# Attention with a gate: row sums of the exponentials taken by ScalarE, P V without its column of ones

## The chip, the core and the metric

The kernel runs on one NeuronCore of a Trainium2 chip. Its engines work side by side, each with its own queue of instructions: TensorE (PE, and PEld for its weight loads), VectorE (DVE), ScalarE (ACT), GpSimd (POOL) and SyncE (SP), which here only issues DMAs. The metric is the device time of one launch in microseconds (us): 788.58 us, the median of three runs (788.07 to 789.41) of the kernel before the change.

## The reference

2048 tokens of width 640 are normalised to `xn`. Attention of 32 heads with 192 columns each looks at a window of the last 512 rows of the key and value caches; its output goes through `wo`, is multiplied by a gate and added to the input:

```python
W = min(4096, max(256, Sk // 4))                 # 512
q = (xn @ wq) per head;  k, v = last W rows of the caches
scores = einsum("bhqd,bhkd->bhqk", q, k) * Dh ** -0.5
p = softmax(scores);  s = einsum("bhqk,bhkd->bhqd", p, v) @ wo
# B: the two tokens with the highest xn @ w_r get a feed-forward update
g = silu(xn + update)
out = x + s * g
```

silu(x) is x times the logistic function of x, which is x (tanh(x/2)/2 + 1/2).

## The kernel before, in words

The queries of two heads (a pair) and 512 tokens make one of 64 steps, and half a step, 256 tokens, is one of 128 blocks. A block has two score tiles, a = 0 and a = 1, of 128 tokens for both heads. `wo` is applied over groups of four heads (two pairs), and adds into `s_acc`.

The order of the work is written out by hand. Blocks 0 to 11 (`HEAD = 12`) are threaded into the start of the kernel by the list `FIRST`, blocks 12 to 125 run in a loop over `BLOCK = "A S0 M0 W m E0 B S1 M1 P E1 l"`, and the list `LAST` holds the end. Each engine executes its instructions in this order. The tokens are:

- A and B: the two halves of a projection of queries for the next step (`q_phase`, L331), and behind B ScalarE's copy of the result out of PSUM (L343).
- S0, S1: the scores of a tile (`scores`, L358). There are two PSUM buffers for score tiles, so S0 of a block needs that E0 of the block before has read its tile, and likewise S1.
- M0, M1: VectorE's row maximum (`row_max`, L363).
- E0, E1: ScalarE's exponentials, two instructions of 128x512 for the two heads (`exps`, L380). Behind each pair SyncE issues a DMA that transposes the result (`pT`, L386).
- W: the product with `wo` for a block six earlier (`w_item`, L467), and two VectorE instructions that add it to `s_acc` (L500).
- P: P V of the block two earlier (`o_products`, L423): 32 matmuls, 16 for each of the two halves of the array (`r`), which run side by side, so 16 pairs. The moving operand is `v_ring[..., 0:Dh + 1]`, 193 columns, of which the last holds a constant 2.0. So column 192 of the result is twice the sum of the exponentials of its row. `o_scaled` takes its reciprocal on VectorE (L430, one instruction for each half) and multiplies it in: one half on ScalarE (L437, two instructions), one on VectorE (L434). Then SyncE issues the transposing DMA of the result (`oT`, L440). The result and W share two PSUM banks.
- m, l: other work that is due in this block, in particular DMA loads, GpSimd's copies (L119, L149) and the steps of the two-token update. Work in `bg` is emitted between the halves of P.

The gate (`gate_of`) is made of a ScalarE tanh (L897) and two GpSimd operations (L898, L899): tanh(x/2) x + x, which is twice silu. The factor two is undone by the 2.0 in the column of ones. It is called once for each of the 16 token tiles in blocks 28, 29, 45 to 53 and 56 to 60, and for the two chosen tokens in blocks 82 and 83. The two-token update is spread to all rows (`y_bc`) and added to the gates from block 85 on (L911, L912).

Of the kernel before, what the change touches and what calls it, by code (L numbers as in the profile page):

```python
# [8 lines left out]
ACT = mybir.ActivationFunctionType  # L9
ALU = mybir.AluOpType  # L10
AX = mybir.AxisListType
ET = mybir.EngineType
FP32 = mybir.dt.float32
# [8 lines left out]
def kernel(ctx, tc, A_x, A_k_cache, A_v_cache, A_wq, A_wo, B_x, B_w_r, B_w_gate, B_w_up, B_w_down, out):  # L22
    nc = tc.nc
    P = 128
# [3 lines left out]
    Dh = A_k_cache.shape[3]  # L28
# [10 lines left out]
    PAIRS = GROUP // 2  # L39
# [4 lines left out]
    scale = float(Dh) ** -0.5  # L44
# [12 lines left out]
    def pool(name, bufs, **kw):  # L57
        return ctx.enter_context(tc.tile_pool(name=name, bufs=bufs, **kw))

    const = pool("const", 1)  # L60
    big = pool("big", 1)
    small = pool("small", 4)
    wq_pool = pool("wq", 3)
    wo_pool = pool("wo", 4)
    kraw_pool = pool("kraw", 1)
# [8 lines left out]
    def f_tile(shape, dtype, name, kind="q"):  # L74
        return banks[kind].tile(shape, dtype, name=name, tag="f")
# [5 lines left out]
    RP, RO, RT, RV, VC = 3, 3, 7, 3, Dh + 8  # L81
    p_ring = big.tile([P, 2, 2, KB, 2, HK], BF16, name="pexp")
    pT_ring = big.tile([P, RP, 2, KB, P], BF16, name="pT")
    o_ring = big.tile([P, RO, CC, 2, HK], BF16, name="o_sb")
    oT_ring = big.tile([P, RT, CC, P], BF16, name="oT")
    v_ring = big.tile([P, RV, KB, VC], BF16, name="v_sb")
# [15 lines left out]
    def half(r):  # L102
        return slice(r * HK, (r + 1) * HK)
# [50 lines left out]
    for _ in range(13):  # L154
# [5 lines left out]
        out=ident_f, in_=ident_f, compare_op=ALU.not_equal, fill=1.0, base=0,  # L160
# [3 lines left out]
    eps_t = const.tile([P, 1], FP32, name="eps_t")  # L164
    nc.vector.memset(eps_t, EPS)
    nc.vector.tensor_copy(out=ident, in_=ident_f)
    nc.gpsimd.memset(v_ring[:, :, :, Dh:Dh + 1], 2.0)

    mv = const.tile([P, NTB, 2], FP32, name="mv")
    rstd = const.tile([P, NTB], FP32, name="rstd")  # L170
# [110 lines left out]
    HEAD = 12  # L281
# [32 lines left out]
    def q_phase(i, cs, ph):  # L314
        g, t5, pr = steps[i]
        if ph == 0:
            if banks["q"] is banks["o"]:
                q_ps = [f_tile([P, W], FP32, "q_ps") for _ in range(2)]
            else:
                q_ps = f_tile([P, 2, W], FP32, "q_ps")  # L320
            q_of[i, cs] = (q_ps, count["S"])
        else:
            assert last_max["S"] > q_of[i, cs][1]
        q_ps = q_of[i, cs][0]
        wq = grp[g][("wq", pr)]
        for dc in range(DC):
            for r in range(2):
                k = r if ph == 0 else 1 - r
                c, tok = (cs[k], slice(t5 * 4, t5 * 4 + 4)) if len(cs) == 2 else (cs[0], slice(t5 * 4 + 2 * k, t5 * 4 + 2 * k + 2))
                n = 512 if len(cs) == 2 else 256  # L330
                mm = nc.tensor.matmul(q_ps[k][:, 0:n] if type(q_ps) is list else q_ps[:, k, 0:n], lhsT=wq[half(r), dc, c:2 * Dh:3], rhs=xnT[half(r), tok, dc, :],  # L331
                                      start=(ph == 0 and dc == 0), stop=(ph == 1 and dc == DC - 1))
                if ph == 1 and dc == 0:
                    tc.add_manual_dep(mm.ins, last_max["ins"].name, mybir.DependencyInfo(mybir.DependencyClass.Sync, mybir.DependencyReason.DATA),
                                      reason="the banks change rows")
        if ph == 1:
            qT = q_tile(i)
            out = qT[:, cs[0]:cs[0] + 2, :] if len(cs) == 2 else qT[:, cs[0], :].rearrange("p (k t) -> p k t", k=2)
            if type(q_ps) is list:
                for k in range(2):  # L340
                    nc.scalar.activation(out=out[:, k], in_=q_ps[k][:, 0:n], func=ACT.Copy, scale=scale)
            else:
                nc.scalar.activation(out=out, in_=q_ps[:, :, 0:n], func=ACT.Copy, scale=scale)  # L343
# [3 lines left out]
    nm_of = {}  # L347

    def scores(b, a):
        i = b // 2  # L350
        g, t5, pr = steps[i]
        u = 2 * (b % 2) + a
        s_of[b, a] = ps_s.tile([P, 2, W], FP32, name="s", tag="sc")
        count["S"] += 1
        s_no[b, a] = count["S"]
        for c in range(3):
            for r in range(2):
                nc.tensor.matmul(s_of[b, a][:, r, :], lhsT=qT_of[i][half(r), c, u * P:(u + 1) * P],  # L358
                                 rhs=grp[g][("kT", pr)][half(r), :, c, :], start=(c == 0), stop=(c == 2))
# [5 lines left out]

    split_of = set()

    p_last = {}

    def p_of(b, a):  # L370
        if b < NB - 1:
            return p_ring[:, b % 2, a]
        if a not in p_last:
            t = wq_pool.tile([P, DC, 2 * Dh], BF16, name="wq_g")
            p_last[a] = t.rearrange("p c d -> p (c d)")[:, 0:KB * P].rearrange("p (k h e) -> p k h e", k=KB, h=2)
        return p_last[a]

    def exps(b, a, split=False):
        for hh in range(2):
            nc.scalar.activation(out=p_of(b, a)[:, :, hh, :].rearrange("p (x j) e -> p x j e", x=2),  # L380
                                 in_=s_of[b, a][:, hh, :].rearrange("p (j e x) -> p x j e", j=NJ, x=2),
                                 func=ACT.Exp, bias=nm_of[b, a][:, hh:hh + 1], scale=1.0)
        if a == 0 and split:
            split_of.add(b)
        if b in split_of:
            nc.sync.dma_start_transpose(out=pT_ring[:, b % RP, a], in_=p_of(b, a).rearrange("p k h e -> p (k h e)"))  # L386
        elif a == 1 and b < NB - 1:
            nc.sync.dma_start_transpose(out=pT_ring[:, b % RP].rearrange("p a k t -> p (a k) t"),
                                        in_=p_ring[:, b % 2].rearrange("p a k h e -> p (a k h e)"))
# [18 lines left out]

    o_of = {}

    def o_products(b, between=None, where="o"):
        g, t5, pr = steps[b // 2]
        if where == "o":
            o_of[b] = [f_tile([P, 2, W // 2], FP32, "o_ps", "o") for _ in range(2)]
        else:
            o_t = f_tile([P, 2, 2, W // 2], FP32, "o_ps") if where == "q" else ps_s.tile([P, 2, 2, W // 2], FP32, name="o_ps", tag="sc")
            o_of[b] = [o_t[:, r] for r in range(2)]
        for a in range(2):
            if a == 1 and between is not None:
                between()  # L420
            for k in range(KB):
                for r in range(2):
                    nc.tensor.matmul(o_of[b][r][:, a, 0:Dh + 1], lhsT=pT_ring[half(r), b % RP, a, k, :],  # L423
                                     rhs=v_ring[half(r), (g * PAIRS + pr) % RV, k, 0:Dh + 1],
                                     start=(k == 0), stop=(k == KB - 1))

    def o_scaled(b, engines):
        rl = small.tile([P, 2, 2], FP32, name="rl")
        for r, e in sorted(enumerate(engines), key=lambda c: c[1]):
            nc.vector.reciprocal(out=rl[:, r], in_=o_of[b][r][:, :, Dh])  # L430
            o_sb = o_ring[:, b % RO, 3 * r:3 * r + 3].rearrange("p c a e -> p a c e")
            src = o_of[b][r][:, :, 0:Dh].rearrange("p a (c e) -> p a c e", e=HK)
            if e == "v":
                nc.vector.tensor_tensor(out=o_sb, in0=src, in1=rl[:, r].unsqueeze(2).unsqueeze(3).to_broadcast([P, 2, 3, HK]), op=ALU.mult)  # L434
            else:
                for a in range(2):
                    nc.scalar.activation(out=o_sb[:, a], in_=src[:, a], func=ACT.Copy, scale=rl[:, r, a:a + 1])  # L437
# [457 lines left out]

    def gate_of(tz, x, y):
        nc.scalar.activation(out=tz, in_=x, func=ACT.Tanh, scale=0.5)  # L897
        nc.gpsimd.tensor_tensor(out=tz, in0=tz, in1=x, op=ALU.mult)  # L898
        nc.gpsimd.tensor_tensor(out=y, in0=tz, in1=x, op=ALU.add)  # L899

    def m_gate(n):
        def f():
# [83 lines left out]
    for b in range(HEAD, NB - 2):  # L986
        for token in BLOCK:
            if token in "AB":
                if b // 2 + 1 < NS:
                    q_phase(b // 2 + 1, ((0, 1), (2,))[b % 2], "AB".index(token))  # L990
            elif token[0] == "S":
                scores(b, int(token[1]))
            elif token[0] == "M":
                row_max(b, int(token[1]))
            elif token[0] == "E":
                exps(b, int(token[1]), split=True)
            elif token == "W":
                w_item(b - LAG)
            elif token == "P":
                def between():  # L1000
                    for f in bg.pop(b, []):
                        f()
                o_item(b - 2, "va", between)
            else:
                for f in mid.pop(b, []) if token == "m" else end.pop(b, []) + loads.pop(b, []):
                    f()

# [64 lines left out]
```

## Time and profile before

| | before |
|---|---|
| median of three runs | 788.58 us |
| the profiled execution | 788.91 us |
| its span, first to last instruction | 787.1 us |
| granted TensorE clock, mean | 0.999 |
| PE busy | 774.5 us (98%) |
| VectorE busy | 578.8 us (74%) |
| ScalarE busy | 527.9 us (67%) |
| GpSimd busy | 339.3 us (43%) |

A row of the groups reads: line, engine, operation, output<-inputs, shapes, count | busy time, mean ns of one | idle time of the engine before them, and what ended it. In the chain of waits each row is a start, a duration and the work that the end of the kernel stood on at that time. In the timeline a row is a start, a duration, and how many instructions were merged into it.

### The profile page before, as it was taken

The page shows a single profiled execution, that of the slowest core. Times are in us where ns is not written, and L with a number is a line of the kernel's source. Part 1 is how long each engine was busy: PE and PEld are TensorE (multiplying, and loading weights), DVE is VectorE, ACT ScalarE, POOL GpSimd, SP SyncE. Part 2 cuts the span into 40 slices and gives each one's busy share as a digit, 9 for nine tenths or more (in the row PEclk, how much of TensorE's full clock was granted, in tenths as well). Part 3 has the DMA queues.
Part 4 walks back from the last instruction along what each step waited for, and adds up shares of the span by engine and source line. Part 5 has one row for each costly group of instructions (what it writes and reads, how often), then busy time and mean ns, then how long its engine had stood idle before and what let it go on. Part 6 is the DMA issues. An engine that isn't in the chain of part 4 may idle for free.

```text
span 787.1 us, 27038 instructions
## 1 busy us (share of the span) xinstructions
PE 774.5 (98%) x11384; PEld 573.3 (73%) x11384; DVE 578.8 (74%) x1068; ACT 527.9 (67%) x956; POOL 339.3 (43%) x281
## 2 busy tenths in 40 slices
PE   8899999999999999999999999999999999999997
PEld 4457677777777777777777777777777777777776
DVE  7898788887787766767767776767767677677675
ACT  6676666667666677767666666766666666666663
POOL 1334110023120236527120101569987696165897
PEclk9999999999999999999999999999999999999999
DMA  9989999899999999999999999999999899999994
GB/s 237 195 174 174 168 193 167 141 195 163 163 211 177 182 201 194 192 171 198 184 194 191 185 216 187 161 193 174 177 168 183 144 170 188 179 193 150 193 190 109
DMA packets 447130, 142.18 MB, mean 181 GB/s; under 512 B 414180, under 2 KB 446438, under 8 KB 447008
## 3 DMA queue, kind: packets, MB, share of 16 engines
q1 hardware_dynamic: 437456, 130.96, 100.5%
q10 hardware_dynamic: 8528, 6.64, 3.4%
q0 software_dynamic: 1024, 2.85, 1.4%
q8 instruction: 89, 1.46, 0.8%
q14 instruction: 33, 0.27, 0.1%
HBM read 40.31 MB, written 2.63 MB: 55 GB/s over the span
## 4 chain that ended last, share of the span: by engine, by line
PE 92%; DVE 3%; DMA 2%; ACT 2%; issue 0%; SPq 0%; DVEq 0%; ACTq 0%
PE w L467 26%; PE q_ps L331 24%; PE o_ps L423 21%; PE s L358 20%; DVE nm L363 1%; PE q_ps L300 1%; ACT pexp L380 1%; DMA oT<-o_sb 1%; DMA x_in<-in_A_x_dram 1%; DMA v_sb<-in_A_v_cache_dram 1%; PE tp L274 0%; ACT o_sb L437 0%; ACT xnT L275 0%; PE gu_ps L821 0%; DVE stats L523 0%
## 5 line engine op out<-in xcount | busy, mean ns | idle before, releaser
L363 DVE TENSOR_REDUCE nm<-s 128x2 f32<-128x1024 f32 x256 | 313.1, 1224 | 137.6 <-PE s L358 135.8
L380 ACT ACTIVATE pexp<-s,nm 128x512 bf16<-128x512 f32 x508 | 321.6, 688 | 95.2 <-DVE nm L363 91.5
L331 PE MATMUL q_ps<-xnT,wq_g 64*128 64x512 bf16 (+1 forms) x2340 | 232.6, 323 | 0.0
L467 PE MATMUL w<-wo_g,oT 64*128 64x320 bf16 x3072 | 231.4, 296 | 0.2
L358 PE MATMUL s<-kT,qT 64*128 64x512 bf16 x1536 | 211.5, 376 | 2.1 <-ACT pexp L380 1.8
L467 PEld LDWEIGHTS <-oT 64*128 64x128 bf16 x3072 | 171.0, 94 | 57.9 <-DMA oT<-o_sb 0.7
L423 PEld LDWEIGHTS <-pT 64*128 64x128 bf16 x4096 | 177.6, 94 | 30.1 <-issue 2.8
L423 PE MATMUL o_ps<-v_sb,pT 64*128 64x193 bf16 x4096 | 195.2, 243 | 2.3 <-DMA pT<-pexp 1.2
L437 ACT ACTIVATE o_sb<-o_ps,rl 128x192 bf16<-128x192 f32 x250 | 91.6, 417 | 130.6 <-DVE rl L430 127.7
L331 PEld LDWEIGHTS <-wq_g 64*128 64x128 bf16 x2340 | 125.8, 99 | 45.8 <-DVE qT L304 0.5
L149 POOL COPY wo_g<-wo_g 64x1920 bf16<-64x1920 bf16 x32 | 57.2, 1792 | 189.4 <-DMA wo_g<-in_A_wo_dram 151.2
L358 PEld LDWEIGHTS <-qT 64*128 64x128 bf16 x1536 | 84.9, 94 | 56.9 <-issue 2.8
L500 DVE TENSOR_TENSOR s_acc<-s_acc,w 128x320 f32<-128x320 f32 x192 | 85.0, 484 | 31.4 <-PE w L467 31.3
L343 ACT ACTIVATE qT<-q_ps 128x1024 bf16<-128x1024 f32 x114 | 92.4, 811 | 7.0 <-PE q_ps L331 0.8
L434 DVE TENSOR_TENSOR o_sb<-o_ps,rl 128x384 bf16<-128x384 f32 x131 | 73.0, 557 | 4.5
L119 POOL COPY k_perm<-k_raw 128x768 bf16<-128x768 bf16 x30 | 24.3, 826 | 93.9 <-DMA k_raw<-in_A_k_cache_dram 67.9
L911 POOL TENSOR_SCALAR yh<-y_bc,oh 128x640 f32<-128x640 f32 x32 | 60.3, 1883 | 5.0 <-DMA y_bc<-y_d 2.3
L912 POOL TENSOR_TENSOR xn<-xn,yh 128x640 bf16<-128x640 bf16 x32 | 44.9, 1404 | 2.7
L898 POOL TENSOR_TENSOR tz<-tz,xn 128x640 f32<-128x640 f32 x16 | 22.4, 1398 | 54.8 <-ACT tz L897 54.8
L430 DVE RECIPROCAL rl<-o_ps 128x2 f32<-128x2 f32 x256 | 30.7, 160 | 11.7 <-PE o_ps L423 6.3
L971 POOL TENSOR_TENSOR s_acc<-s_acc,x_fin 128x640 f32<-128x640 f32 x16 | 22.4, 1398 | 10.9 <-DMA x_fin<-in_A_x_dram 9.9
L899 POOL TENSOR_TENSOR xn<-tz,xn 128x640 bf16<-128x640 f32 x16 | 22.4, 1398 | 1.3
(141 smaller groups left out, 275.8 us busy)
## 6 DMA issues: line engine op xcount, KB each, us to landing
wo_g<-in_A_wo_dram SPq DMA_DIRECT2D x32, 240.0 KB, 4.2
k_raw<-in_A_k_cache_dram SPq DMA_DIRECT2D x32, 192.0 KB, 3.5
v_sb<-in_A_v_cache_dram SPq DMA_DIRECT2D x32, 192.0 KB, 4.1
wq_g<-in_A_wq_dram SPq DMA_DIRECT2D x14, 288.0 KB, 4.0
pT<-pexp SPq DMA_TRANSPOSE x246, 4.1
wq_g<-in_A_wq_dram SPq DMA_DIRECT2D x14, 192.0 KB, 2.9
x_fin<-in_A_x_dram SPq DMA_DIRECT2D x16, 160.0 KB, 3.6
oT<-o_sb SPq DMA_TRANSPOSE x126, 3.6
```

What stands on the lines that cost most here:

```text
L149: nc.gpsimd.tensor_copy(out=grp[g][("wo", pr)][half(1), cs, :], in_=grp[g][("wo", pr)][half(0), cs, :])
L331: mm = nc.tensor.matmul(q_ps[k][:, 0:n] if type(q_ps) is list else q_ps[:, k, 0:n], lhsT=wq[half(r), dc, c:2 * Dh:3], rhs=xnT[half(r), tok ...
L343: nc.scalar.activation(out=out, in_=q_ps[:, :, 0:n], func=ACT.Copy, scale=scale)
L358: nc.tensor.matmul(s_of[b, a][:, r, :], lhsT=qT_of[i][half(r), c, u * P:(u + 1) * P], rhs=grp[g][("kT", pr)][half(r), :, c, :], start=(c = ...
L363: rm = nc.vector.tensor_reduce(out=nm_of[b, a], in_=s_of[b, a], axis=AX.X, op=ALU.max, negate=True)
L380: nc.scalar.activation(out=p_of(b, a)[:, :, hh, :].rearrange("p (x j) e -> p x j e", x=2), in_=s_of[b, a][:, hh, :].rearrange("p (j e x) - ...
L423: nc.tensor.matmul(o_of[b][r][:, a, 0:Dh + 1], lhsT=pT_ring[half(r), b % RP, a, k, :], rhs=v_ring[half(r), (g * PAIRS + pr) % RV, k, 0:Dh ...
L434: nc.vector.tensor_tensor(out=o_sb, in0=src, in1=rl[:, r].unsqueeze(2).unsqueeze(3).to_broadcast([P, 2, 3, HK]), op=ALU.mult)
L437: nc.scalar.activation(out=o_sb[:, a], in_=src[:, a], func=ACT.Copy, scale=rl[:, r, a:a + 1])
L467: nc.tensor.matmul(w_ps[r][:, 0:cs.stop - cs.start], lhsT=oT_ring[half(r), bs[pr] % RT, c, :], rhs=grp[g][("wo", pr)][half(r), c, cs], sta ...
L500: nc.vector.tensor_tensor(out=acc, in0=acc, in1=src, op=ALU.add)
L911: nc.gpsimd.tensor_scalar(out=yh, in0=M["y_bc"][:, j, :], scalar1=M["oh"][:, n, j:j + 1], scalar2=None, op0=ALU.mult)
```

## The change

From block 12 on `exps` passes `accum_out`: each ScalarE instruction writes, beside the exponentials, their sum over its 512 elements into one column of a small tile `l` (five buffers, for the two token tiles and two heads of a block). VectorE takes one reciprocal of the four columns of `l` (`o_factor`), in token m of the block in which P of that `l` stands; in the list `LAST` it is taken in `o_scaled`. P V from block 12 on has 192 columns. The ScalarE and VectorE multiplications of `o_scaled` read the result of P and this reciprocal. Blocks 0 to 11 keep the column, which now holds 1.0. The gate becomes x (tanh(x/2)/2 + 1/2): the first GpSimd operation is a `tensor_scalar` with two constants in place of a `tensor_tensor`, and the second one multiplies where it added. The order of the matmuls and of the DMA issues is as it was.

```diff
-    nc.gpsimd.memset(v_ring[:, :, :, Dh:Dh + 1], 2.0)
+    nc.gpsimd.memset(v_ring[:, :, :, Dh:Dh + 1], 1.0)
...
     def exps(b, a, split=False):
+        if b >= HEAD and a == 0:
+            l_of[b] = sums.tile([P, 2, 2], FP32, name="l")
         for hh in range(2):
             nc.scalar.activation(out=p_of(b, a)[:, :, hh, :].rearrange("p (x j) e -> p x j e", x=2),
                                  in_=s_of[b, a][:, hh, :].rearrange("p (j e x) -> p x j e", j=NJ, x=2),
-                                 func=ACT.Exp, bias=nm_of[b, a][:, hh:hh + 1], scale=1.0)
+                                 func=ACT.Exp, bias=nm_of[b, a][:, hh:hh + 1], scale=1.0,
+                                 accum_out=l_of[b][:, hh, a:a + 1] if b >= HEAD else None)
...
+    def o_factor(b):
+        rl_of[b] = small.tile([P, 2, 2], FP32, name="rl")
+        nc.vector.reciprocal(out=rl_of[b], in_=l_of[b])
+
     def o_products(b, between=None, where="o"):
+        n = Dh if b >= HEAD else Dh + 1
...
-                    nc.tensor.matmul(o_of[b][r][:, a, 0:Dh + 1], lhsT=pT_ring[half(r), b % RP, a, k, :],
-                                     rhs=v_ring[half(r), (g * PAIRS + pr) % RV, k, 0:Dh + 1],
+                    nc.tensor.matmul(o_of[b][r][:, a, 0:n], lhsT=pT_ring[half(r), b % RP, a, k, :],
+                                     rhs=v_ring[half(r), (g * PAIRS + pr) % RV, k, 0:n],
                                      start=(k == 0), stop=(k == KB - 1))
 
     def o_scaled(b, engines):
-        rl = small.tile([P, 2, 2], FP32, name="rl")
+        if b >= HEAD and b not in rl_of:
+            o_factor(b)
+        rl = rl_of[b] if b >= HEAD else small.tile([P, 2, 2], FP32, name="rl")
         for r, e in sorted(enumerate(engines), key=lambda c: c[1]):
-            nc.vector.reciprocal(out=rl[:, r], in_=o_of[b][r][:, :, Dh])
+            if b < HEAD:
+                nc.vector.reciprocal(out=rl[:, r], in_=o_of[b][r][:, :, Dh])
...
     def gate_of(tz, x, y):
         nc.scalar.activation(out=tz, in_=x, func=ACT.Tanh, scale=0.5)
-        nc.gpsimd.tensor_tensor(out=tz, in0=tz, in1=x, op=ALU.mult)
-        nc.gpsimd.tensor_tensor(out=y, in0=tz, in1=x, op=ALU.add)
+        nc.gpsimd.tensor_scalar(out=tz, in0=tz, scalar1=0.5, scalar2=0.5, op0=ALU.mult, op1=ALU.add)
+        nc.gpsimd.tensor_tensor(out=y, in0=tz, in1=x, op=ALU.mult)
...
             else:
+                if token == "m" and b - 2 >= HEAD:
+                    o_factor(b - 2)
```

More of the change, by code (lines that the diff above doesn't have):

```diff
@@ L62 @@
     small = pool("small", 4)
+    sums = pool("sums", 5)
     wq_pool = pool("wq", 3)
@@ L366 @@
     split_of = set()
+    l_of = {}
+    rl_of = {}
     p_last = {}
```

## The prediction

> **What bounds the kernel now.** I read the engines' busy time first, then the chain of waits, then the timeline of two blocks and of the end.
>
> ```profile
> span 787.1 us, 27038 instructions
> PE 774.5 (98%) x11384; PEld 573.3 (73%) x11384; DVE 578.8 (74%) x1068; ACT 527.9 (67%) x956; POOL 339.3 (43%) x281
> PE 92%; DVE 3%; DMA 2%; ACT 2%; issue 0%; SPq 0%; DVEq 0%; ACTq 0%
> ```
>
> The chain stands on matmuls for 92% of the span. A busy PE need not be PE at its pace, so the stages themselves have to be looked at. This is the chain inside the loop, and one row of it from a worse place:
>
> ```profile
> 156.34 0.65 PE s L358 x6
> 156.99 1.63 PE w L467 x24
> 158.62 1.08 PE q_ps L331 x10
> 159.70 0.65 PE s L358 x6
> 160.34 1.33 PE o_ps L423 x32
> 161.68 0.55 PE q_ps L331 x10
> ...
> 216.25 1.80 PE w L467 x24
> ```
>
> One stage follows the other with nothing between. Matmuls come in pairs, one for each half of the array. W has 12 pairs of 320 columns in 1.63 us, 136 ns a pair; the projection has 5 pairs of 512 columns in 1.08 us, 216 ns; P has 16 pairs of 193 columns in 1.33 us, 83 ns. From P to W that is 53 ns for 127 columns, from W to the projection 80 ns for 192: 0.417 ns for a column both times. So these stages go by their columns, and PE has no waits in the loop except for single cases such as 1.80 us for W at 216.25. Nearly all that other engines do is hidden behind PE, and the change is worth what it takes from PE's columns, unless it makes another engine late.
>
> **P with 192 columns.** From block 12 on there are 116 blocks with 16 pairs each: 116 x 16 x 0.417 ns = 0.77 us less on PE, all of it on the path. The two ends are 0 (the pair is paced by something else than columns, a rival below) and 0.80 (time in proportion to columns, 1.33 us / 193 for each). I take 0.77, because the slope comes out the same from two intervals.
>
> **The sums on ScalarE.** A sum needs an instruction that reads it out. This kernel has such reads in its start, behind row sums of another kind:
>
> ```profile
> 58.45 1.26 ACT L380 ACTIVATE pexp<-s,nm 128x512 bf16<-128x512 f32 x2
> 59.59 0.83 ACT L538 ACTIVATE xn<-x_in,sums 128x640 bf16<-128x640 bf16 x1
> 60.31 0.20 ACT L538 ACTIVATION_READ_ACCUMULATOR xn<-x_in,sums 128x1 f32 x1
> 60.40 0.83 ACT L538 ACTIVATE xn<-x_in,sums 128x640 bf16<-128x640 bf16 x1
> ```
>
> The read is recorded with 0.20 us but overlaps on both sides. Two exponentials of 1.26 us are followed after 1.14 us, so an instruction overlaps the next by 0.12. Without the read, the one at 59.59 would be followed after 0.83 - 0.12 = 0.71 us; it was followed after 0.81. The read costs 0.10 us. It can't cost less than nothing, since no work leaves ScalarE with it; the upper end is the whole 0.20 with the overlaps on both of its sides lost, about 0.40. I take 0.10, the measured one: 0.2 us for each pair of exponentials, 0.4 us a block. Whether that is hidden is read from a pair of blocks in which the tanh of a gate makes ScalarE busiest:
>
> ```profile
> 304.35 0.24 DVE L430 RECIPROCAL rl<-o_ps 128x2 f32<-128x2 f32 x2
> 304.56 0.42 ACT L437 ACTIVATE o_sb<-o_ps,rl 128x192 bf16<-128x192 f32 x1 [0.54 <-DVE rl L430]
> 304.88 0.41 ACT L437 ACTIVATE o_sb<-o_ps,rl 128x192 bf16<-128x192 f32 x1
> 305.18 1.27 ACT L380 ACTIVATE pexp<-s,nm 128x512 bf16<-128x512 f32 x2
> 305.34 1.81 PE L467 MATMUL w<-wo_g,oT 64*128 64x320 bf16 x24
> 306.87 1.27 ACT L380 ACTIVATE pexp<-s,nm 128x512 bf16<-128x512 f32 x2 [0.43 <-DVE nm L363]
> 308.03 0.60 ACT L343 ACTIVATE qT<-q_ps 128x512 bf16<-128x512 f32 x1
> 308.51 0.74 ACT L897 ACTIVATE tz<-xn 128x640 f32<-128x640 bf16 x1
> 309.49 1.26 PE L331 MATMUL q_ps<-xnT,wq_g 64*128 64x512 bf16 x10
> 309.71 0.24 DVE L430 RECIPROCAL rl<-o_ps 128x2 f32<-128x2 f32 x2
> 309.92 0.73 ACT L437 ACTIVATE o_sb<-o_ps,rl 128x192 bf16<-128x192 f32 x2 [0.66 <-DVE rl L430]
> 311.22 2.06 PE L467 MATMUL w<-wo_g,oT 64*128 64x320 bf16 x24
> ```
>
> E1 at 305.18 gets 0.2 longer and starts up to 0.2 earlier (below), so it ends where it did; behind it ScalarE waits 0.43 us for the row maximum, and E0 at 306.87 starts as before. E0's 0.2 moves the copy of the queries from 308.03 to 308.23; it ends at 308.83, and PE needs its bank back at 309.49. The tanh ends at 309.45 in place of 309.25, and ScalarE waited until 309.92 for the reciprocal, 0.66. What stands behind the exponentials (the DMA pT that SyncE issues, the score buffer that PE refills) gets the 0.2 as well: the buffer read from 306.87 to 308.14 is refilled by the scores ahead of W at 311.22, 0.65 us earlier, at 310.57, which leaves 2.4 us. If this cover were gone, 0.2 a pair would be 0.4 us a block or 46 us in all; it isn't. Cost on the path: 0.
>
> **The reciprocal.** It leaves the place between P and `o_scaled`. ScalarE's L437 starts 0.21 us after the first L430 (304.35, 304.56), and without it starts that much earlier: when P is done. VectorE's half gains the 0.24 of two. The result is out of PSUM 0.2 us sooner, W finds its banks free sooner (at 305.34 they had been free for 0.05 us: 304.88 + 0.41 = 305.29), and SyncE may issue oT sooner. PE did not wait there, so this is worth nothing in the loop, but it pays for E1's longer time. The new reciprocal of four columns, 0.12 to 0.24 us by the row of two, lies on VectorE in front of the maximum M1:
>
> ```profile
> L363 DVE TENSOR_REDUCE nm<-s 128x2 f32<-128x1024 f32 x256 | 313.1, 1224 | 137.6 <-PE s L358 135.8
> ```
>
> VectorE waits for scores for 135.8 us ahead of these 256, 0.53 us each, which covers it; the sum it reads was written a block earlier. 0.
>
> **The gate.** GpSimd's first operation changes its kind:
>
> ```profile
> L898 POOL TENSOR_TENSOR tz<-tz,xn 128x640 f32<-128x640 f32 x16 | 22.4, 1398 | 54.8 <-ACT tz L897 54.8
> L911 POOL TENSOR_SCALAR yh<-y_bc,oh 128x640 f32<-128x640 f32 x32 | 60.3, 1883 | 5.0 <-DMA y_bc<-y_d 2.3
> L185 POOL TENSOR_SCALAR xn<-x_in,rstd,nmr 128x640 bf16<-128x640 bf16 x7 | 6.4, 919 | 6.4 <-DVE nmr L189 6.4
> ...
> 522.01 0.83 POOL L119 COPY k_perm<-k_raw 128x768 bf16<-128x768 bf16 x1 [0.42 <-DMA k_raw<-in_A_k_cache_dram]
> 541.58 1.54 SPq L123 DMA_TRANSPOSE kT<-k_perm  x1
> ```
>
> It is between 0.48 us shorter (L185) and 0.49 longer (L911, the nearer in type) than 1.40. With 16 gates GpSimd waits 54.8 us for the tanh, 3.4 each, which covers it. With the two of blocks 82 and 83 the spread of the update and GpSimd's copies of keys behind it come up to 1 us later; the transposing DMA that reads them is issued 18.7 us after them. 0.
>
> **The end.** Here the chain leaves PE for once:
>
> ```profile
> 770.39 0.61 PEld L405 LDWEIGHTS <-wq_g 64*128 64x128 bf16 x32
> 770.69 0.17 DVE L430 RECIPROCAL rl<-o_ps 128x2 f32<-128x2 f32 x1 [0.40 <-PE o_ps L423]
> 770.89 0.73 ACT L437 ACTIVATE o_sb<-o_ps,rl 128x192 bf16<-128x192 f32 x2 [0.50 <-DVE rl L430]
> 770.94 1.51 PE L423 MATMUL o_ps<-v_sb,pT 64*128 64x193 bf16 x32
> 771.66 0.17 DVE L430 RECIPROCAL rl<-o_ps 128x2 f32<-128x2 f32 x1 [0.80 <-ACT o_sb L437]
> 771.87 0.56 DVE L434 TENSOR_TENSOR o_sb<-o_ps,rl 128x384 bf16<-128x384 f32 x1
> 772.57 1.81 PE L467 MATMUL w<-wo_g,oT 64*128 64x320 bf16 x24
> ```
>
> P of block 126 at 770.94 takes 1.33 us, so W could start at 772.27; it starts at 772.57, since its bank is freed by the VectorE half of block 125 at 771.87 + 0.56 = 772.43. Both reciprocals go from in front of it, 0.20 and 0.21 us. Then the bank is free at 772.02, ahead of PE: 0.30 us gained (0 if something else holds W).
>
> **Sum.** 0.77 + 0.30 = 1.07 us less. The profiled execution took 788.91, of which the span is 787.1; it would take 787.84. It lies 0.33 above the median of the runs, so against the median of 788.58 I say 787.5, which is 0.14% faster. About 0.2% (1.6 us) is what a measurement of this kernel can tell from no change, so this falls within it.
>
> **Rivals.**
>
> The column buys nothing. P could be paced by its weight loads, of which there are as many after as before:
>
> ```profile
> L423 PEld LDWEIGHTS <-pT 64*128 64x128 bf16 x4096 | 177.6, 94 | 30.1 <-issue 2.8 <-DMA pT<-pexp 1.4 <-DMA v_sb<-in_A_v_cache_dram 0.7
> ```
>
> For it speaks that a load lasts 94 ns, longer than the 83 ns of a pair. Against it: the 32 loads at 770.39 were done in 0.61 us, 38 ns a pair, so loads overlap each other, and P lies on the line of the other stages. Then only the end is gained: 788.3. The Trainium skill has such a rule (TensorE: Matmul & The Clock Gate, "Back-to-back issue gap" and "LDWEIGHTS"): the spacing in a stream of loads and matmuls is set by both, and a load takes its columns over 1.2 in ns. An estimate from that page for the 128 columns here is 107 ns, 1.71 us for 16 in a row; the trace's 1.33 us does not agree.
>
> Waits shrink too. Banks are free 0.2 us sooner and oT may be issued sooner; W at 216.25 lost 0.17 us and W at 311.22 lost 0.25 (2.06 against 1.81). If both vanish and other small ones with them, 0.5 to 0.8 us more are gained: 786.9. Against it: W at 311.22 waits for a DMA, and SyncE issues that in its own order.
>
> Slower: the read does not overlap in front of exponentials. At 0.40 us each, E1 ends 0.8 - 0.2 later, 0.17 more than the 0.43 it may; E0 ends 0.17 + 0.8 later, and the copy of the queries at 309.60, 0.11 past the 309.49 at which PE wants the bank. The point is 4 reads = 0.43 + 0.2 + 0.86, or 0.37 us a read. With 58 pairs of blocks that is 6 us, and the tanhs add to it: 794. Against it is the measured 0.10.
>
> **How the numbers follow.** My forecast has 0.64, with 787.0 to 788.1 as its own range; the column that buys nothing 0.10; waits that shrink 0.16; the late ScalarE, or another engine made late in its manner, 0.10. The range from 786.5 to 788.9 takes in the first three and leaves out the last and a little below. Faster by over 0.2%, under 787.0: 0.18, the third with the lower edge of the first. Slower: 0.12, the fourth and a little of the scatter. Within: 0.70.
>
> **What the profile will show.** P of 32 matmuls at 1.32 to 1.33 us in the chain; a read of about 0.2 us behind each exponential, pairs of exponentials 1.45 to 1.5 us from start to end of the read; L437 waiting for PE and no longer for L430; ScalarE busy near 73% (464 reads of 0.10 us more); W in the end at 772.27 less what was gained before. I am wrong if the query copies end after PE wants their bank, if the scores wait for ScalarE in the loop, or if P keeps 83.3 ns a pair to the last digit.

## The result

The changed kernel takes 785.51 us (median; 785.36 to 786.62) beside 788.80 before. The ratio is 0.9961, with an interval from 0.9948 to 0.9973: faster by 0.39%, some 3.1 us (3.3 between the medians), where 1.07 us were forecast. The range began at 786.5, so the time lies below it.

The page of the changed kernel, its first lines, and the rows of the groups that the change touches:

```profile
span 784.0 us, 27247 instructions
...
PE 771.7 (98%) x11384; PEld 572.0 (73%) x11384; DVE 561.2 (72%) x952; ACT 566.2 (72%) x1420; POOL 327.1 (42%) x281
...
L452 ACT ACTIVATE o_sb<-o_ps,rl 128x192 bf16<-128x192 f32 x250 | 91.6, 418 | 97.3 <-PE o_ps L435 88.3 <-DVE rl L445 6.9 <-DMA pT<-pexp 1.0
...
L386 ACT ACTIVATION_READ_ACCUMULATOR pexp<-s,nm 128x1 f32 x460 | 94.0, 204 | 0.0
...
L386 ACT ACTIVATION_READ_ACCUMULATOR wq_g<-s,nm 128x1 f32 x4 | 0.8, 210 | 0.0
...
L913 POOL TENSOR_SCALAR tz<-tz 128x640 f32<-128x640 f32 x16 | 11.7, 728 | 63.7 <-ACT tz L912 63.7
```

All 464 reads are there: 460, and four whose exponentials go to a buffer of another name. ScalarE's half of P's result waits for PE now and hardly for a reciprocal; ScalarE is busy 72% of the span. GpSimd's first gate operation takes 0.73 us.

The chain of waits in the loop, around the same two places as before:

```profile
156.03 0.65 PE s L359 x6
156.68 1.63 PE w L482 x24
158.31 1.08 PE q_ps L332 x10
159.39 0.65 PE s L359 x6
160.04 1.32 PE o_ps L435 x32
161.36 0.55 PE q_ps L332 x10
...
215.38 1.63 PE w L482 x24
```

P takes 1.32 us, and W at 215 is back at 1.63 us from 1.80. To say what made up the 3.1 us, I divided each profile at the same matmuls: the head up to the first score matmul of block 13, the loop from there to the first one of block 126 (113 blocks), and the tail. Single waits are those matmuls of the loop that start over 40 ns later behind the one before than nearly all of their kind do, summed over the excess. All from the start times of matmuls, in us:

| | P columns, reciprocal | head | loop | single waits in it | loop without them | tail | span |
|---|---|---|---|---|---|---|---|
| before | 193, behind P | 91.40 | 668.85 | 1.01 | 667.84 | 26.89 | 787.14 |
| changed | 192, early | 91.28 | 666.26 | 0.40 | 665.86 | 26.50 | 784.04 |

Of 3.10 us the loop without single waits gives 1.98, single waits 0.61, the tail 0.39 and the head 0.12. The experiments take the loop and the tail apart.

### The profile page after: what moved, and what is told of

It reads as the page before. It is cut to its first block, busy times and chain, and to the rows that moved or that the text cites. A ratio compares the mean times of both kernels' runs of the same rounds, so it can differ in the third digit from the quotient of the medians.

```text
span 784.0 us, 27247 instructions
## 1 busy us (share of the span) xinstructions
PE 771.7 (98%) x11384; PEld 572.0 (73%) x11384; DVE 561.2 (72%) x952; ACT 566.2 (72%) x1420; POOL 327.1 (42%) x281
## 4 chain that ended last, share of the span: by engine, by line
PE 93%; DVE 4%; ACT 2%; DMA 0%; issue 0%; DVEq 0%; ACTq 0%
PE w L482 26%; PE q_ps L332 24%; PE o_ps L435 21%; PE s L359 20%; DVE nm L364 1%; PE q_ps L301 1%; ACT pexp L386 1%; DMA x_in<-in_A_x_dram 0%; DVE stats L538 0%; DVE o_sb L449 0%; ACT xnT L276 0%; DVE qT L305 0%; PE gu_ps L836 0%; PE tp L275 0%; DVE stats L248 0%
## 5 line engine op out<-in xcount | busy, mean ns | idle before, releaser
L386 ACT ACTIVATE pexp<-s,nm 128x512 bf16<-128x512 f32 x508 | 342.6, 688 | 94.7 <-DVE nm L364 91.0
L435 PE MATMUL o_ps<-v_sb,pT 64*128 64x192 bf16 (+1 forms) x4096 | 193.7, 243 | 2.8 <-DMA pT<-pexp 1.6
L386 ACT ACTIVATION_READ_ACCUMULATOR pexp<-s,nm 128x1 f32 x460 | 94.0, 204 | 0.0
L913 POOL TENSOR_SCALAR tz<-tz 128x640 f32<-128x640 f32 x16 | 11.7, 728 | 63.7 <-ACT tz L912 63.7
```

Of the source, the lines that this page charges most:

```text
L435: nc.tensor.matmul(o_of[b][r][:, a, 0:n], lhsT=pT_ring[half(r), b % RP, a, k, :], rhs=v_ring[half(r), (g * PAIRS + pr) % RV, k, 0:n], star ...
```

## The experiments

Three kernels were built between the two: the gate alone, then the sums without their use, then the early reciprocal with P still at 193 columns; the changed kernel is the last step.

**The gate alone.** The kernel before with

```diff
-    nc.gpsimd.memset(v_ring[:, :, :, Dh:Dh + 1], 2.0)
+    nc.gpsimd.memset(v_ring[:, :, :, Dh:Dh + 1], 1.0)
...
-        nc.gpsimd.tensor_tensor(out=tz, in0=tz, in1=x, op=ALU.mult)
-        nc.gpsimd.tensor_tensor(out=y, in0=tz, in1=x, op=ALU.add)
+        nc.gpsimd.tensor_scalar(out=tz, in0=tz, scalar1=0.5, scalar2=0.5, op0=ALU.mult, op1=ALU.add)
+        nc.gpsimd.tensor_tensor(out=y, in0=tz, in1=x, op=ALU.mult)
```

> The kernel before with the new gate alone (and the column of ones at 1.0). GpSimd's first operation went from 1.40 to 0.73 us. Theory: it is hidden, so 788.8 us within 0.3, and the single long W stages of the loop (1.80 us at 216, 2.06 at 311) stay. Rival: a shorter GpSimd operation relieves these waits, up to 0.6 us: 788.2.

**The sums, not used.** The same, with `accum_out` in `exps` from block 12 on; P and the reciprocals as before:

```diff
+                                 accum_out=l_of[b][:, hh, a:a + 1] if b >= HEAD else None)
...
         rl = small.tile([P, 2, 2], FP32, name="rl")
             nc.vector.reciprocal(out=rl[:, r], in_=o_of[b][r][:, :, Dh])
```

> The kernel before with the new gate and with the sums taken on ScalarE but not used: P keeps 193 columns and the reciprocals are taken from PSUM behind P as before. Against the run with 193 columns it differs in the place of the reciprocal alone, against the gate alone in the reads of ScalarE. Theory: the early reciprocal frees W's banks sooner and that is where 1 to 1.5 us came from, so this is 788.8 us or up to 0.5 more, with the start of W behind the scores alternating as before (about 0.20 and 0.21 us behind the last score matmul). Rival: the reads themselves shift the DMA issues into better places, then 787.5 or less.

**The early reciprocal, 193 columns.** The changed kernel with

```diff
-        n = Dh if b >= HEAD else Dh + 1
+        n = Dh + 1
```

> The changed kernel with P at 193 columns again (the last is not used); all else of the change stays. It tells what the column alone is worth. Theory now: TensorE takes columns in twos, so 193 cost as much as 194, and the P stage of 32 matmuls goes back from 1.32 us to 1.333 us: 116 blocks x 13.4 ns = 1.55 us, 787.1 us beside 785.5. Theory of the prediction, 0.417 ns for one column: 786.3 us, and the P stage at 1.327 us or lower. If the sums and the early reciprocal did nothing, the time would be that of before, 788.8; I expect the other 1.6 us to stay gained.

What the three gave, beside 789.08 us for the kernel before on the same chip:

| | median | ratio to before, interval | head | loop | single waits | loop without | tail |
|---|---|---|---|---|---|---|---|
| gate alone | 788.87 | 0.9998 (0.9988 to 1.0007) | 90.94 | 669.16 | 1.35 | 667.81 | 26.78 |
| with sums, unused | 789.11 | 0.9996 (0.9985 to 1.0008) | 93.23 | 668.25 | 0.48 | 667.77 | 26.87 |
| early reciprocal, 193 | 787.74 | 0.9985 (0.9975 to 0.9994) | 91.34 | 668.35 | 1.00 | 667.35 | 26.52 |
| changed | | | 91.28 | 666.26 | 0.40 | 665.86 | 26.50 |

The row of the changed kernel is its profile from the result above; it did not run beside the other three. The gate and the reads on ScalarE change the loop without single waits by 0.03 and 0.04 us: they are hidden. The two long W stages, expected to stay with the gate alone, are not in its profile; P at 309 us waited 0.87 us there instead, for the transposing DMA of `pT`.

The place of the reciprocal is worth 0.42 us in the loop and 0.35 in the tail, the column 1.49 in the loop: 13.2 ns for each of 113 blocks, 0.82 ns for each pair of matmuls. That is two columns at 0.417 ns, not one. These steps repeat: over all profiles of these kernels and of those below with equal widths, the loop without single waits is 667.77 to 667.84 us with 193 columns and the reciprocal behind P, 667.35 and 667.36 with 193 and the early one, and 665.86 to 665.89 with 192.

The medians differ by more than the parts found in the profiles: 1.37 us for the place of the reciprocal, of which 0.77 are located, and 2.0 to 2.2 for the column (the changed kernel has 785.51 above and 785.75 below) where 1.55 were expected. What the executions without a profile waited for is not known. The heads differ by up to 2.3 us between kernels whose first 12 blocks do the same, so one profile tells nothing of a head.

**P at several widths.** The changed kernel, with the columns behind 192 set and not used:

```diff
-        n = Dh if b >= HEAD else Dh + 1
+        n = Dh + ((0, 1, 2, 3, 4, 5, 6, 8)[b // 2 % 8] if b >= HEAD else 1)
...
-    nc.gpsimd.memset(v_ring[:, :, :, Dh:Dh + 1], 1.0)
+    nc.gpsimd.memset(v_ring[:, :, :, Dh:VC], 1.0)
```

> The changed kernel with P at 192, 193, 194, 195, 196, 197, 198 and 200 columns, by step modulo 8 (the columns past 192 are not used), so that one trace gives the price of each. In twos: the stage of 32 matmuls lasts 1.320 us with 192, 1.333 with 193 and 194, 1.347 with 195 and 196, 1.360 with 197 and 198, 1.373 with 200. One by one at 0.417 ns: 192 at 1.320, then 6.7 ns more for each column, 1.327 at 193 and 1.333 at 194. Paced by the weight loads: the same for all.

The timeline of PE, start of P and of the projection behind it, at 198, 200, 192, 193, 194, 195 and 196 columns:

```profile
106.55 1.54 PE L435 MATMUL o_ps<-v_sb,pT 64*128 64x198 bf16 x32
107.91 1.25 PE L332 MATMUL q_ps<-xnT,wq_g 64*128 64x512 bf16 x10
...
112.99 1.55 PE L435 MATMUL o_ps<-v_sb,pT 64*128 64x200 bf16 x32
114.36 0.72 PE L332 MATMUL q_ps<-xnT,wq_g 64*128 64x256 bf16 x10
...
131.04 1.50 PE L435 MATMUL o_ps<-v_sb,pT 64*128 64x192 bf16 x32
132.36 1.26 PE L332 MATMUL q_ps<-xnT,wq_g 64*128 64x512 bf16 x10
...
142.79 1.51 PE L435 MATMUL o_ps<-v_sb,pT 64*128 64x193 bf16 x32
144.12 1.26 PE L332 MATMUL q_ps<-xnT,wq_g 64*128 64x512 bf16 x10
...
154.56 1.51 PE L435 MATMUL o_ps<-v_sb,pT 64*128 64x194 bf16 x32
155.89 1.26 PE L332 MATMUL q_ps<-xnT,wq_g 64*128 64x512 bf16 x10
...
166.34 1.53 PE L435 MATMUL o_ps<-v_sb,pT 64*128 64x195 bf16 x32
167.68 1.26 PE L332 MATMUL q_ps<-xnT,wq_g 64*128 64x512 bf16 x10
...
178.13 1.52 PE L435 MATMUL o_ps<-v_sb,pT 64*128 64x196 bf16 x32
179.48 1.26 PE L332 MATMUL q_ps<-xnT,wq_g 64*128 64x512 bf16 x10
```

1.36, 1.37, 1.32, 1.33, 1.33, 1.34 and 1.35 us. Over all such stages of the trace the medians in ns are 1320 at 192; 1333 and 1333 at 193 and 194; 1347 and 1346 at 195 and 196; 1360 and 1360 at 197 and 198; 1373 at 200 (13 to 26 stages each). The steps are of 13.3 ns and come at each second column: the columns go in twos. The load-paced rival, by which all widths take the same time, falls with it. The whole took 789.46 us in one execution, with more columns on the average; its time is not compared.

**A wait that comes and goes.** The kernel with the early reciprocal and 193 columns had one long wait in its loop, 0.80 us of W at 116. The timeline of VectorE and GpSimd there:

```profile
112.27 0.17 DVE L420 RECIPROCAL rl<-l 128x4 f32<-128x4 f32 x1
112.35 2.32 DVE L723 SCALAR_TENSOR_TENSOR junk<-xn,wr_bc 128x640 bf16<-128x640 bf16 x1
...
114.60 1.22 DVE L364 TENSOR_REDUCE nm<-s 128x2 f32<-128x1024 f32 x1
115.73 0.54 DVE L449 TENSOR_TENSOR o_sb<-o_ps,rl 128x384 bf16<-128x384 f32 x1
...
112.21 1.78 POOL L150 COPY wo_g<-wo_g 64x1920 bf16<-64x1920 bf16 x1 [17.39 <-DMA wo_g<-in_A_wo_dram]
```

And of W, which that delayed:

```profile
116.33 1.81 PE L482 MATMUL w<-wo_g,oT 64*128 64x320 bf16 x24 [0.64 <-DVE o_sb L449]
```

The product with w_r (0.8 us else) lasted 2.32 us where GpSimd's copy had begun 0.14 us ahead of it; the row maximum and VectorE's half of P's result moved behind it, and W waited for its bank. The profile with mixed columns has it too: there the copy began 0.05 us ahead, the product lasted 2.41 us and W at 116 waited 0.87. In five other profiles the same copy began behind the product, by 0.28 us (twice) and by 1.09 to 1.20 (three times). It starts when a DMA lands, so the order can change from one execution to the next. Two runs followed: the changed kernel again, and one with these products at the end of their blocks.

> The changed kernel once more, beside the three next ones. With P at 193 columns the median was 787.7 us and the profile held one wait of 0.80 us of W at 116 us: VectorE's product with w_r (0.8 us else) lasted 2.32 us, since GpSimd's copy of wo had begun 0.2 us ahead of it. The changed kernel's profile did not hold it. Theory: it depends on when a DMA lands and comes in some executions of each kernel; then this one is at 785.5 or up to 0.8 above, in two clusters. Rival: the change removes it for good, then 785.5 within 0.3.

```diff
-        spot(b).append(m_r(n))
+        end[b].append(m_r(n))
```

> The changed kernel with VectorE's products with w_r always at the end of their block (token l), behind the half of P's result that VectorE takes out of PSUM, in place of token m for every second one. A long product then can't hold W's banks. Theory: no wait of W at 116 us in any execution, 785.4 us and less spread than the changed kernel. Rival: the product now delays the row maximum M0 of the next block, which has 0.4 to 0.7 us to spare in front of it: up to 0.4 us for each of 13 products that do not fit, 788 at worst.

Beside 789.12 us for the kernel before, the changed kernel came to 785.75 us (785.50 to 787.68, ratio 0.9966, 0.9954 to 0.9978), with the products at the end 785.67 (785.44 to 786.12, ratio 0.9957, 0.9945 to 0.9969). Both profiles are free of the long product, and their loops without single waits last 665.86 and 665.89 us. Three of the eight times of the first lie between 786.8 and 787.7, and none of the six of the second. That fits a wait that comes in some executions, but these three are 1.0 to 1.9 us above the others where 0.8 was expected, and none of them has a profile, so the product is not shown as their cause. The next run speaks against it as the only one: it has the products at the end too, and its times spread over 1.9 us. The second is not measurably faster.

**The column with that wait out of the way.** The run before, with

```diff
-        n = Dh if b >= HEAD else Dh + 1
+        n = Dh + 1
```

> The run before, but P at 193 columns. With the wait at 116 us out of both, the difference of the two is the column alone. Columns in twos: 1.55 us slower than the run before, 786.9 to 787.0. One column of 0.417 ns: 0.77 us slower, 786.2.

787.69 us (787.11 to 789.03, ratio 0.9984, 0.9976 to 0.9993): 2.02 us slower by the medians, 1.67 by the lowest times. The loop without single waits is 667.36 against 665.89 us, 1.47 more, which is again the price of two columns. Both are above the 1.55 expected, and the medians have half a microsecond more than the loop; what the executions without a profile waited for is not to be seen.

**The sums in all blocks.** To see whether the start wants them too:

```diff
-    nc.gpsimd.memset(v_ring[:, :, :, Dh:Dh + 1], 1.0)
...
-        if b >= HEAD and a == 0:
+        if a == 0:
...
-                                 accum_out=l_of[b][:, hh, a:a + 1] if b >= HEAD else None)
+                                 accum_out=l_of[b][:, hh, a:a + 1])
...
-        n = Dh if b >= HEAD else Dh + 1
+        n = Dh
```

> The products with w_r at the end, and the sums on ScalarE in all 128 blocks, with P at 192 columns from the first on and no column of ones. Blocks 0 to 11 have 12 x 13.4 ns = 0.16 us less on TensorE, but ScalarE is busier there and gets 48 reads of 0.1 us. If the start hides them, 785.2; if they lie on the path there, up to 4.8 us slower; I expect 785.2 to 786.

787.48 us (786.91 to 789.47, ratio 0.9984, 0.9976 to 0.9993), 1.8 us slower than with the sums from block 12 on and outside of what was expected. The loop is the same (666.33 us against 666.30); the head is 92.57 us against 91.54. So in the profiles most of the loss is in the start, but since heads scatter by as much, it is not shown that the reads are its cause.

**How far ScalarE's cover reaches.** The changed kernel with one, then two copies behind each exponential (range 2 in place of 1), which serve nothing:

```diff
+            for _ in range(1 if b >= HEAD else 0):
+                nc.scalar.copy(out=junk_a, in_=ident[:, 0:112])
```

> The changed kernel with a ScalarE copy of 128x112 behind each exponential from block 12 on, which serves nothing; about 0.2 us each (a 128x128 one took 0.31 us, of which 0.12 overlap). With the reads that is about three times what the change added. In the changed kernel E0 follows 0.42 us behind E1, and the copy of the queries ends 0.68 us ahead of PE's want of its bank. Two copies of 0.2 move it by 0.4: theory, ScalarE still fits, 785.7 us within 0.7. Rival: ScalarE was already close to late, then each pair of blocks loses 0.1 us or more, 791 or later.

> The same with two such copies, about 0.4 us behind each exponential. The prediction's point, 0.37 us a read, is passed: E0 starts 0.4 late, the copy of the queries ends 1.2 late where 0.68 were to spare, 0.5 us for each of 57 pairs of blocks. Theory: ScalarE is the bound now, 800 to 820 us, with the score or projection stages waiting for it. Rival: it still fits, 786.

The first took 789.81 us in one execution, 4 us more than the changed kernel, where no change was expected. Busy times by stretch of the loop, the run with one copy and then the second profile of the changed kernel:

```profile
66.00:200.00 134.00, 133.85 (x1980) 101.61 (x1977) 105.96 (x187) 108.68 (x312) 24.84 (x30) 1.00 1.07 173
200.00:500.00 300.00, 297.51 (x4471) 217.80 (x4468) 205.13 (x341) 255.55 (x767) 72.10 (x69) 1.00 1.14 188
500.00:760.00 260.00, 260.00 (x3900) 204.89 (x3897) 176.51 (x268) 220.13 (x669) 189.61 (x131) 1.00 1.05 176
```

```profile
66.00:200.00 134.00, 133.85 (x1980) 99.31 (x1977) 105.61 (x187) 95.76 (x236) 24.45 (x30) 1.00 1.05 174
200.00:500.00 300.00, 300.00 (x4533) 223.70 (x4530) 208.31 (x346) 223.76 (x576) 75.96 (x71) 1.00 1.13 191
500.00:760.00 260.00, 260.00 (x3900) 204.85 (x3897) 176.47 (x266) 189.38 (x493) 189.15 (x132) 1.00 1.04 175
```

The columns are the stretch, its length, then busy time and number of instructions of PE, PEld, VectorE, ScalarE and GpSimd. Outside of 200 to 500 us PE is as busy and runs as many matmuls as without the copies. A copy makes the next exponential start 0.17 us later (0.851 us from start to start in the median, against 0.677 with the reads alone and 0.585 before), and there this is hidden. Between 200 and 500 PE runs 62 matmuls fewer.

Set side by side matmul by matmul, the loops of these two profiles differ by 3.75 us, and all of it lies in ten of the 113 blocks. None of the ten is one of the blocks 28, 29 and 45 to 53, each with a tanh, which took the same time to 0.01 us. In blocks 43, 54, 65, 72 and 79 (1.3 us together) matmuls of the two-token update stand between the halves of P, in the PSUM bank of the projection, and wait 0.2 to 0.3 us for the query copy to read it out. In blocks 63, 64 and 68 (0.8 us) a projection waits for that copy; in 64 and 68 ScalarE had issued a DMA of the update's weights just ahead of its exponentials. In blocks 34 and 58 (1.6 us) W waits for the transposed result:

```profile
PE w L485 <- DMA oT<-o_sb: 1.3, 2, 0.9
```

In block 34 that is not a late ScalarE: the DMA was issued 2.32 us after the start of block 33, against 2.50 and 2.61 in the two profiles of the changed kernel, and landed later. So with 0.27 us more for each exponential (read and copy) the cover holds in nearly all blocks, those with a tanh between 45 and 53 among them, and ends first where the update's matmuls want the bank of the query copy.

With two copies it took 853.74 us, far more than the 800 to 820 expected. Who waited for whom:

```profile
PE q_ps L333 <- ACT qT L345: 34.9, 64, 1.1
...
PE gu_ps L839 <- ACT qT L345: 3.0, 3, 1.0
```

It is the wait that the prediction named for a late ScalarE, PE's wait for the query copies. The loop is 64.5 us longer than in the second profile of the changed kernel: behind P the projection starts 0.56 us later in each of 107 blocks, 59.4 us, and the update's matmuls take the other 5. The expectation had 0.4 us for two copies; they delay the next exponential by 0.50 (1.174 us from start to start), and ScalarE was busy for 90% of the span.

## Why the prediction was wrong, point by point

None of the four cases reached 785.5 us; the nearest, waits that shrink, had 786.9. Of the 2.03 us that the two profiles have beyond the 1.07 forecast, the column gives 0.72, the reciprocal in the loop 0.42, single waits 0.61, the head 0.12, the tail 0.09 and the rest of the loop 0.07.

**The column, the step that failed most.** The term was mis-sized: 0.77 us for 116 x 16 columns, and 116 x 13.2 ns = 1.53 us by what the loop showed. The working took "one column" for 1/127 of the difference between P and W, and found 0.417 ns twice. It had divided a rounded 53 ns. With the start times of the trace, P's pair lasts 83.3 ns and W's 135.8 (1.630 us / 12), and 52.5 / 127 is 0.413, while 52.5 / 126 is 0.417: the third digit said that P costs as 194 columns. The upper end given for it, 0.80, was worked out from proportion and so was too low by half.

**"PE did not wait there, so this is worth nothing in the loop".** This step of the reciprocal was wrong. It was read off that W's bank had been free for 0.05 us when W began. But before, the last score matmul was followed by W after 0.196 and 0.208 us in alternating blocks, and in 56 of the 57 blocks of the second kind W started 50 to 52 ns behind the end of ScalarE's half: that gap is the time from the release to the start, and W was waiting. With the sums taken but the reciprocal still behind P the two kinds are there as before (0.196 and 0.208); with it early both have a median of 0.196, and W starts 229 ns behind the release where it had 51. 12 ns in 57 blocks are 0.68 us. W itself is 3 ns longer there now (1.630 us against 1.627), which leaves 0.51 beside the 0.42 us that moving the reciprocal gave. The timeline of the changed kernel at the same place shows the bank free 0.23 us ahead:

```profile
303.07 0.42 ACT L452 ACTIVATE o_sb<-o_ps,rl 128x192 bf16<-128x192 f32 x1 [0.34 <-PE o_ps L435]
...
303.39 0.41 ACT L452 ACTIVATE o_sb<-o_ps,rl 128x192 bf16<-128x192 f32 x1
...
304.03 1.79 PE L482 MATMUL w<-wo_g,oT 64*128 64x320 bf16 x24
```

**The end.** Right: 0.35 us from the early reciprocal against 0.30 forecast. P of block 126 now has W behind it without a wait, 768.20 + 1.32 = 769.52:

```profile
767.95 0.73 ACT L452 ACTIVATE o_sb<-o_ps,rl 128x192 bf16<-128x192 f32 x2
...
768.20 1.50 PE L435 MATMUL o_ps<-v_sb,pT 64*128 64x192 bf16 x32
...
768.72 0.56 DVE L449 TENSOR_TENSOR o_sb<-o_ps,rl 128x384 bf16<-128x384 f32 x1 [1.06 <-ACT o_sb L452]
...
769.52 1.81 PE L482 MATMUL w<-wo_g,oT 64*128 64x320 bf16 x24
```

**The reads on ScalarE.** Right in price, and in cover for this change. A read is recorded with 0.20 us and delays the next exponential by 0.09: from start to start 0.677 us in the median over the loop, where it was 0.585. Here 0.68 and 0.67:

```profile
299.70 0.69 ACT L386 ACTIVATE pexp<-s,nm 128x512 bf16<-128x512 f32 x1 [0.96 <-DVE nm L364]
300.28 0.19 ACT L386 ACTIVATION_READ_ACCUMULATOR pexp<-s,nm 128x1 f32 x1
300.38 0.68 ACT L386 ACTIVATE pexp<-s,nm 128x512 bf16<-128x512 f32 x1
...
303.69 0.69 ACT L386 ACTIVATE pexp<-s,nm 128x512 bf16<-128x512 f32 x1
304.26 0.21 ACT L386 ACTIVATION_READ_ACCUMULATOR pexp<-s,nm 128x1 f32 x1
304.36 0.69 ACT L386 ACTIVATE pexp<-s,nm 128x512 bf16<-128x512 f32 x1
```

The point of 0.37 us a read lies between what was tried: in blocks 45 to 53, each with a tanh, 0.27 us an exponential cost nothing and 0.59 cost 8.6 us. What the prediction left out is the update's matmuls, which want the bank of the query copy ahead of the projection and were late with 0.27 already.

**The gate.** Hidden, as said. The bounds given for GpSimd's first operation did not hold: 0.73 us lies below the lower one, 0.92 (L185).

**The rivals.** The column that buys nothing is refuted: P's time moves with its width. The estimate of 1.71 us by the rule of the Trainium skill that stood beside it (TensorE: Matmul & The Clock Gate, "Back-to-back issue gap" and "LDWEIGHTS") does not fit either, since P took 1.320 to 1.373 us. The late ScalarE did not come. Waits that shrink did, for 0.61 us of the 3.10 in the two profiles. By kind, the three profiles with the reciprocal behind P have 1.01, 1.35 and 0.48 us of single waits, the three at 193 or mixed columns with it early 1.00, 0.85 and 0.40, and the four at 192 in the loop 0.40, 0.22, 0.41 and 0.47. This hangs on landings of DMAs in single executions, and how much of it belongs to the change stays open.

## What to carry to other kernels

In a loop where TensorE's stages follow each other without a gap, take the price of a column from start times to the last digit and try it on two widths that differ by one: 193 columns cost what 194 do. A bank that becomes free a few hundredths of a microsecond ahead of the matmul that wants it counts as a wait until a run shows otherwise. An accumulating read of 0.1 us on an engine off the path cost nothing here, but its cover must be looked for at every place that wants that engine's results, the rare ones too: with a copy more behind each exponential, nine blocks with a tanh lost nothing, and five in which a matmul of the update wants the bank of the query copy lost 0.2 to 0.3 us each.

## What the runs showed of the hardware that was not expected

TensorE takes the columns of a moving operand of bf16 in twos (64 partitions, into PSUM in float32): 13.3 ns for 16 pairs of matmuls at each second column from 192 to 200.

A VectorE instruction with two inputs in SBUF (0.8 us) took 2.32 us when a GpSimd copy in SBUF had begun 0.14 us before it. In the kernel before the order was the other way round, and there the copy was the longer one, with the product at 112.34 to 113.16:

```profile
112.34 0.82 DVE L708 SCALAR_TENSOR_TENSOR junk<-xn,wr_bc 128x640 bf16<-128x640 bf16 x1
...
112.62 2.17 POOL L149 COPY wo_g<-wo_g 64x1920 bf16<-64x1920 bf16 x1 [17.47 <-DMA wo_g<-in_A_wo_dram]
```

The Trainium skill says so (SBUF — State Buffer, "Who interferes with whom"): such a VectorE instruction and a GpSimd instruction that reads SBUF exclude each other, and the order of issue decides who waits. The durations agree to 0.15 us: the copy of 1.78 us ended at 113.99, and 114.67 less that is 0.68 us, nearly the whole product of 0.82; in the other order the copy overlapped the product for 0.54 us and took 0.39 us longer.

A GpSimd operation on 128x640 float32 with two constants took 0.73 us, one with a scalar from memory for each partition (L911) 1.88, and one with two tensors 1.40.
